# Attention with token and channel mixing on one core: third chunk's scores in plain float32, key and query splits and token-weight conversion moved

## The chip, the cores and the metric

The program runs on one core of one Trainium2 chip. A core has TensorE (PE, matrix products; its weight loads are listed as PEld), VectorE (DVE), ScalarE (ACT), GpSimd (POOL) and SyncE (SP, which here issues nearly all transfers). Each engine works through its own queue in the order in which the code issues to it, and waits at an instruction until what that instruction needs is there. The metric is the device time of one execution in microseconds (us).

## The reference

Three parts follow one another, for a batch of 2 and a sequence of 448. Attention with 12 heads of 64 mixes the heads before and after the softmax:

```
scores = scale * q @ k.T                      # per head
scores = einsum('bhij,hg->bgij', scores, w_pre)
attn   = exp(scores - max); attn = attn / (sum + 1e-9)
attn   = einsum('bhij,hg->bgij', attn, w_post)
x      = attn @ v                             # (2, 448, 768)
```

Then a mixer (`u = x + relu(x.T @ w_tok1) @ w_tok2` over the sequence, `x = u + relu(u @ w_ch1) @ w_ch2` over the channels), and a gated block with tanh gelu, a normalisation and a product over the sequence (`w_in`, `w_sg`, `w_out`). Inputs of attention are float32. The four mixer weights, `w_in` and `w_out` arrive as float64.

## The kernel before

**Numbers in two parts.** Most products are made of three: a float32 value is split into a high part in the type float32r (a cast) and a low part (the difference), and high*high, high*low, low*high are summed in PSUM (`mm3`, lines 626 to 631). The first scores of batch 0 are made otherwise, by one product of plain float32 operands.

**Attention in blocks.** Rows of the scores are taken in chunks of 120, 120, 120 and 88 for each batch, 8 chunks `(b, c)`. A chunk is worked in blocks of 10 rows by 12 heads (120 partitions), 90 blocks in all (12, 12, 12, 9 for each batch). For a block `i`: its scores come by DMA from the tile `S` into `P` (`b_dma`), ACT makes the high part `Ph` (`b_high`, line 391), POOL the low part `Pl` (`b_low`, line 397), PE multiplies by `w_pre` in three products (`b_pre`, 403 to 405), DVE takes the maximum `nm` (407), ACT the exponential `E` with its sum (411), DVE makes `rc` and its reciprocal `rr` (418, 421), POOL scales `w_post` by it into `wt` (424), PE multiplies `E` by `wt` in four products into `post` (436), and DVE copies that into `AT` (444).

**The order is written out by hand.** One loop runs over steps `i` from -8 to 89 (lines 555 to 612). Step `i` issues, for different blocks: `wt(i+1)`, the load of `P(i+8)`, `Ph(i+6)` and `Pl(i+6)`, `rc(i+2)`, the copy of `post(i-1)` to `AT`, `rr(i+2)`, then whatever the table `extra` holds for that step, then `pre(i+4)` and `post(i)`, and behind these the products `av` of a finished chunk with `v`, two heads' pairs at a time (lines 447 to 462, 588 to 592). So on POOL a step is `wt(i+1)`, `Pl(i+6)`, and the extras.

**The extras** are set by `add(step, ...)` (lines 509 to 548): the scores `qk` of the next chunk (345 to 365), the split of a pair of key heads into `KH` (DVE cast, 328) and `KL` (POOL, 329) by `kprep`, the split of three pairs of query heads into `QH` (DVE, 339) and `QL` (POOL, 340) by `qprep`, and loads. `load_const_late` issues a small DMA, builds the identity matrix `ident` on POOL (two instructions of masks.py) and a memset on DVE. A step with `qk` or `av` in it has more work for PE than one without.

**Weights.** `w_conv` (120 to 162) turns one piece of a float64 weight into two float32r parts. It is a generator: ACT takes `Abs` of the upper words into `cv` (117, issued one piece ahead by `w_abs`), DVE needs four instructions (135, 137, 139, 141), ACT casts to the high part (154 or 158) and DVE (156) or POOL (159) makes the low part; between them it yields. `pump(n)` advances it by `n` steps, as far as buffers allow. Pieces 0 and 1 are `w_tok1`, 2 and 3 `w_tok2`, from 4 on `w_ch1`. The load of piece `i+3` is issued when piece `i` is done, since there are three buffers `raw`. Pumping starts ten steps before the end of the loop, one step at a time, and goes on between the last six `av` of the tail loop (614 to 616).

**After the loop** `tok1(0)` and `tok1(1)` (660 to 678) multiply the transposed `x` by `w_tok1`; the transposes `xps` (PE, ACT cast 473 to `xh`, DVE 474 to `xl`) of batch 0 are made in the last four steps of the loop, those of batch 1 in `tok1(0)`. `rounds(n, w)` advances the waiting evacuations and pumps `w` each time. `tok2`, the channel mixing and the last block follow; `need(i)` pumps until a piece is ready.

Of the kernel before, what the change touches and what calls it, by code (L numbers as in the profile page):

```python
# [19 lines left out]
LD, LS, LP, LN = 8, 6, 4, 2  # L20
# [10 lines left out]
def tile_kernel(ctx, tc, q, k, v, w_pre, w_post, w_tok1, w_tok2, w_ch1, w_ch2,  # L31
# [88 lines left out]
    def w_conv(i):  # L120

        src, pr, a, n, scale, dst = pieces[i]
        r = wstate["raw"][i]
        if src.dtype == F32:
            f = r.bitcast(F32)
        else:

            r = r.rearrange("p a (n t) -> p a n t", t=2)
            lo, hi = r[:, :, :, 0], r[:, :, :, 1]
            if i not in wstate["abs"]:  # L130
                w_abs(i)
                yield
            f = wstate["abs"].pop(i)
            fi = f.bitcast(U32)
            nc.vector.tensor_scalar(f, f, MIN_HI, MAX_HI, op0=ALU.max, op1=ALU.min)
            yield
            nc.vector.tensor_scalar(fi, fi, 3, 0x3FFFFFFF, op0=ALU.logical_shift_left, op1=ALU.bitwise_and)
            yield
            nc.vector.scalar_tensor_tensor(fi, lo, 29, fi, op0=ALU.logical_shift_right, op1=ALU.bitwise_or)  # L139
            yield  # L140
            nc.vector.scalar_tensor_tensor(fi, hi, 0xC0000000, fi, op0=ALU.bitwise_and, op1=ALU.bitwise_or)  # L141

            w_abs(i + 1)
        yield
        if dst is None:
            h = wpool.tile([P, WC], F32R, tag="wth", name=f"wh{i}", bufs=WB)
            l = wpool.tile([P, WC], F32R, tag="wtl", name=f"wl{i}", bufs=WB)
            dst = pieces[i][5] = (h[:pr, :a * n].rearrange("p (a n) -> p a n", a=a),
                                  l[:pr, :a * n].rearrange("p (a n) -> p a n", a=a))
        elif callable(dst):  # L150
            dst = pieces[i][5] = dst()
        if i in p_t1:

            nc.scalar.copy(dst[0], f)
            yield
            nc.vector.tensor_tensor(dst[1], f, f32(dst[0]), op=ALU.subtract)
        elif scale is None:
            nc.scalar.copy(dst[0], f)  # L158
            nc.gpsimd.tensor_tensor(dst[1], f, f32(dst[0]), op=ALU.subtract)  # L159
        else:  # L160
            nc.scalar.activation(dst[0], f, AF.Copy, scale=scale)
            nc.vector.scalar_tensor_tensor(dst[1], f, scale, f32(dst[0]), op0=ALU.mult, op1=ALU.subtract)
# [134 lines left out]
    QG = 3  # L297
# [47 lines left out]
    def qk(b, c, i, pools=None, copies=(nc.scalar.copy, nc.scalar.copy)):  # L345

        s0, n = CH[c]
        if i == 0:
            SS[b, c] = big(f"S{b}_{c}", F32)[:120].rearrange("p (h s) -> p h s", h=H)
        ps = [pool.tile([P, 512], F32, tag=tag, name=f"qk{b}_{c}_{2 * i + j}")  # L350
              for j, (pool, tag) in enumerate(pools or [(psA, "A")] * 2)]
        cs = slice(i % QG * n, (i % QG + 1) * n)
        if b == 0 and (c < 2 or c == 2 and i < QG):

            terms = [(qn[b, c, i // QG], KX[b, i])]
        else:
            (qh, ql), (kh, kl) = QQ[b, c, i // QG], KK[b, i]
            terms = [(qh, kh), (qh, kl), (ql, kh)]
        for t, (x, y) in enumerate(terms):
            for j in range(2):  # L360
                rows = slice(64 * j, 64 * j + 64)
                nc.tensor.matmul(ps[j][:n, :S], lhsT=x[rows, cs], rhs=y[rows], start=(t == 0),  # L362
                                 stop=(t == len(terms) - 1))
        for j in range(2):
            copies[j](SS[b, c][:n, 2 * i + j, :], ps[j][:n, :S])
# [112 lines left out]
    def add(step, fn, *a):  # L478
        extra.setdefault(step, []).append((fn, a))
# [29 lines left out]
    for i in range(NP):  # L509
# [3 lines left out]
        else:  # L513
            add(2 * i - 9, qk, 0, 1, i)

        add(2 * i + 11 if i < QG else 3 * i - 5, kprep, 0, i, nc.vector.tensor_copy, nc.gpsimd)
    add(-LP, turn_over, 4)
    add(6, qprep, 0, 2, 1)
    for g in range(NQ):
        add(1 + 6 * g, load_q, 0, 3, g)  # L520
    for hp in range(NP):
        add(3 + hp, load_v, 0, hp)
    add(LD + 2, load_const_late)

    for x in range(2, NCH):
        b, c = chunks[x]
# [4 lines left out]
        for i in range(NP):  # L531
# [5 lines left out]
            else:  # L537
                add(s_, qk, b, c, i)
            if nxt and i % QG == QG - 1:
                add(s_ + 3, qprep, *nxt, i // QG)  # L540
                if nxt2:
                    add(s_ + 4, load_q, *nxt2, i // QG)
            if nxt and nxt[1] == 0:
# [4 lines left out]
                add(s_ + 1 + i % 2, kprep, nxt[0], i, nc.vector.tensor_copy, nc.gpsimd)  # L548

    todo = []  # L550
    NS = S // KP
    X, RX = {}, {}
    turns = [(0, s, ch) for ch in range(2) for s in range(NS)]

    for i in range(-LD, NB):
# [25 lines left out]
        if i >= 0:  # L581
# [3 lines left out]
                b_turn(i)  # L585

            nb = len(chunk_blocks(CH[c][1]))
            while todo and NP - len(todo) < 2 * ((j + nb // 6) * 3 // nb):
                av(*todo[0])
                if todo[0][1] == len(CH) - 1 and b:  # L590
                    add(i + 1, load_v, b, todo[0][2])
# [16 lines left out]
        if i + LP >= NB:  # L608
            for _ in range(2):
                turn(psB.tile([P, 512], F32, tag="B", name=f"xps0_{len(turns)}"), *turns.pop(0))  # L610
        if i + LS + 4 >= NB:

            pump(1)
    while todo:
        av(*todo.pop(0))
        pump(2)
    actx.close()


# [37 lines left out]
    with ExitStack() as mctx:  # L657
        mp = mctx.enter_context(tc.tile_pool(name="tok", bufs=1, reuse_waits="tile"))
        RR = {}
        def tok1(b, turns=()):  # L660
# [4 lines left out]
            for tt in range(TOK // P):  # L665
                ts = slice(tt * P, (tt + 1) * P)
                for ch in range(2):
# [5 lines left out]
                    for _ in range(2):  # L673
                        if turns:
                            s, tch = turns.pop(0)
                            turn(bank(f"xps1_{s}_{tch}"), 1, s, tch)
                    rounds(2, 2 - b)
            RR[b] = (rh, rl, got)

        def tok2(b):  # L680
# [305 lines left out]
```

## Time and profile before

| | |
|---|---|
| time, median of 3 runs | 553.54 us (553.32 to 556.22) |
| profiled execution, its own time | 552.82 us |
| its span | 550.9 us |
| PE busy | 537.3 us, 98% (3630 products) |
| PE weight loads busy | 477.5 us, 87% |
| DVE, ACT, POOL busy | 394.8 (72%), 274.0 (50%), 280.8 us (51%) |
| granted TensorE clock, mean | 0.999 of full speed |

The page counts an engine as busy while it executes. The share is an average over the whole program; the stretches by stage are read from the rows further down. A product in float32 stands in the profile as two records, so the four products of `post` are 8 records, and a pair of plain score products for one pair of heads is 4.

### The profile page before, as it was taken

To read this page: it belongs to the slowest core of one execution; us is meant where nothing else is said; L and a number is where in the kernel's file an instruction comes from. 1 tells how busy PE (TensorE), PEld (TensorE's weight loads), DVE (VectorE), ACT (ScalarE), POOL (GpSimd) and SP (SyncE) were. 2 spreads that over 40 slices of the span, in tenths; PEclk is the share of its full clock that TensorE was granted. 3 is DMA by queue.
4 is the path that set the end of the run, shared out by engine and by line. 5 is a ranking of instruction groups with operands and counts; after the bars stand their busy time and mean duration, and the time that the engine had idled before them with its cause. 6 is when DMAs were issued, how large, how long until landed. Compare 5 with 4: busy or idle time off the path is not lost.

```text
span 550.9 us, 10089 instructions
## 1 busy us (share of the span) xinstructions
PE 537.3 (98%) x3630; PEld 477.5 (87%) x3630; DVE 394.8 (72%) x789; ACT 274.0 (50%) x582; POOL 280.8 (51%) x295
## 2 busy tenths in 40 slices
PE   9999999999999999789999999999999999999997
PEld 5677888888888888789999999999999998888986
DVE  4787877667676677886356876778887974798972
ACT  4875757666676765454333443433233343455320
POOL 0699997767676763035522223244444545057600
PEclk9999999999999999999999999999999999999999
DMA  6564444424422541342032434334353323201322
GB/s 204 187 209 143 149 141 108 123 81 149 157 100 97 165 125 35 125 147 75 0 113 71 142 97 150 117 114 153 115 166 102 96 90 111 67 1 47 106 101 101
DMA packets 26340, 63.12 MB, mean 115 GB/s; under 512 B 2914, under 2 KB 18834, under 8 KB 26290
## 3 DMA queue, kind: packets, MB, share of 16 engines
q1 hardware_dynamic: 26002, 62.10, 34.5%
q8 instruction: 29, 0.48, 0.3%
q10 hardware_dynamic: 288, 0.37, 0.2%
q14 instruction: 21, 0.17, 0.1%
HBM read 40.36 MB, written 2.75 MB: 78 GB/s over the span
## 4 chain that ended last, share of the span: by engine, by line
PE 85%; DVE 6%; issue 2%; POOL 2%; ACT 2%; DMA 1%; SPq 0%; POOLq 0%; ACTq 0%
PE post L436 11%; PE av L454 7%; PE qk L362 5%; PE c1ps L630 5%; PE c2ps L630 5%; PE c2ps L629 5%; PE c1ps L629 5%; PE c2ps L631 5%; PE c1ps L631 5%; PE pre L403 4%; PE pre L405 3%; PE pre L404 3%; PE ups L629 2%; PE ups L631 2%; PE ups L630 2%
## 5 line engine op out<-in xcount | busy, mean ns | idle before, releaser
L397 POOL TENSOR_TENSOR Pl<-P,Ph 120x448 fp32r<-120x448 f32 x87 | 100.2, 1152 | 54.7 <-ACT Ph L391 51.7
L159 POOL TENSOR_TENSOR wl<-cv,wh 128x768 fp32r<-128x768 f32 x28 | 52.5, 1875 | 122.3 <-ACT wh L158 88.1
L436 PEld LDWEIGHTS post<-wt,E 120*112 120x112 f32 x720 | 86.2, 176 | 7.9 <-POOL wt L424 3.2
L436 PE MATMUL post<-wt,E 120*112 120x120 f32 x720 | 88.8, 266 | 2.2 <-POOL wt L424 1.5
L411 ACT ACTIVATE E<-pre,nm 120x448 f32<-120x448 f32 x90 | 57.5, 638 | 55.4 <-DVE rc L418 45.6
L444 DVE COPY AT<-post 112x480 f32<-112x480 f32 x90 | 58.6, 651 | 6.0 <-PE post L436 1.6
L407 DVE TENSOR_REDUCE nm<-pre 120x1 f32<-120x448 f32 x90 | 54.9, 610 | 4.1 <-PE pre L405 2.9
L139 DVE SCALAR_TENSOR_TENSOR cv<-raw,cv 128x768 uint32<-128x768 uint32 (+3 forms) x44 | 54.0, 1227 | 1.2
L630 PE MATMUL c1ps<-ul,wh 128*128 128x448 f32 x144 | 52.9, 367 | 0.0
L630 PE MATMUL c2ps<-r1l,wh 128*128 128x448 f32 x144 | 52.9, 367 | 0.0
L391 ACT CAST Ph<-P 120x448 fp32r<-120x448 f32 x90 | 52.2, 580 | 0.9 <-DMA P<-S 0.8
L629 PE MATMUL c1ps<-uh,wh 128*128 128x448 f32 x144 | 52.3, 363 | 0.0
L629 PE MATMUL c2ps<-r1h,wh 128*128 128x448 f32 x144 | 52.3, 363 | 0.0
L631 PE MATMUL c1ps<-uh,wl 128*128 128x448 f32 x144 | 52.0, 361 | 0.0
L631 PE MATMUL c2ps<-r1h,wl 128*128 128x448 f32 x144 | 52.0, 361 | 0.0
L117 ACT ACTIVATE cv<-raw 128x768 f32<-128x768 f32 (+3 forms) x44 | 36.2, 823 | 27.4 <-POOL wl L159 18.3
L454 PE MATMUL av<-AT,vn 112*64 112x120 f32 (+1 forms) x768 | 42.0, 263 | 0.3 <-DVE xT L462 0.3
L158 ACT CAST wh<-cv 128x768 fp32r<-128x768 f32 x28 | 23.4, 836 | 36.6 <-DVE cv L141 32.8
L403 PE MATMUL pre<-Ph,wpl 120*120 120x448 f32 x90 | 40.5, 450 | 0.6 <-DVE rc L418 0.4
L141 DVE SCALAR_TENSOR_TENSOR cv<-raw,cv 128x768 uint32<-128x768 uint32 (+3 forms) x44 | 40.2, 914 | 1.1
L454 PEld LDWEIGHTS av<-AT,vn 112*64 112x64 f32 x768 | 37.1, 137 | 3.1 <-PE av L454 0.5
L652 DVE SCALAR_TENSOR_TENSOR r1l<-c1ps,r1h 128x448 fp32r<-128x448 f32 x24 | 15.0, 624 | 31.2 <-ACT r1h L650 31.2
(202 smaller groups left out, 1220.3 us busy)
## 6 DMA issues: line engine op xcount, KB each, us to landing
P<-S SPq DMA_DIRECT2D x90, 210.0 KB
raw<-in_w_ch_dram SPq DMA_DIRECT2D x24, 768.0 KB
raw<-in_w_v_dram SPq DMA_DIRECT2D x6, 512.0 KB
raw<-in_w_u_dram SPq DMA_DIRECT2D x4, 768.0 KB
raw<-in_w_out_dram SPq DMA_DIRECT2D x6, 512.0 KB
vn<-in_v_dram SPq DMA_DIRECT2D x12, 224.0 KB
out_dram<-xT SPq DMA_DIRECT2D x12, 224.0 KB
qn<-in_q_dram SPq DMA_DIRECT2D x10, 180.0 KB
```

What stands on the lines that cost most here:

```text
L139: nc.vector.scalar_tensor_tensor(fi, lo, 29, fi, op0=ALU.logical_shift_right, op1=ALU.bitwise_or)
L159: nc.gpsimd.tensor_tensor(dst[1], f, f32(dst[0]), op=ALU.subtract)
L397: eng.tensor_tensor(lo, st[i]["P"], f32(st[i]["h"]), op=ALU.subtract)
L403: nc.tensor.matmul(ps[:BW, :S], lhsT=wpl, rhs=hi, start=True, stop=False)
L407: nc.vector.tensor_reduce(out=nm, in_=ps[:BW, :S], axis=AX.X, op=ALU.max, negate=True)
L411: nc.scalar.activation(e, ps[:BW, :S], AF.Exp, bias=nm, scale=1.0, accum_out=sm)
L436: nc.tensor.matmul(ps[:KP, r * BW:(r + 1) * BW], lhsT=e[:, r * KP:(r + 1) * KP], rhs=wt, start=True, stop=True)
L444: nc.vector.tensor_copy(AT[b, c][:, :, :, j * IB:(j + 1) * IB], src)
L454: nc.tensor.matmul(ps[64 * j:64 * j + 64, :cols], lhsT=vn[b, hp][:, j, r, :], rhs=AT[b, c][:, r, 2 * hp + j, :cols], start=(r == 0), stop= ...
L629: nc.tensor.matmul(ps, lhsT=lh, rhs=rh, start=(start and i == 0), stop=False)
L630: nc.tensor.matmul(ps, lhsT=lh, rhs=rl, start=False, stop=False)
L631: nc.tensor.matmul(ps, lhsT=ll, rhs=rh, start=False, stop=(stop and i == n - 1))
```

## The change

In the scores of chunk `(0, 2)`, the three pairs of heads 3 to 5 are now made by one product of plain float32 operands each, as those of 0 to 2 already were (`qk`: `c < 3`). The query split `qprep(0, 2, 1)` is gone. The key splits of batch 0 (`kprep`), which stood at steps 11, 13, 15, 4, 7, 10 for heads' pairs 0 to 5, stand at 5, 9, 15, 17, 21, 23. The query splits of chunk `(0, 3)` move from 12 and 16 to 13 and 19, `load_const_late` from 10 to 27.

The conversion of the token weights starts earlier: three pump steps ahead of the `av` of a step, from step 75 on (75, 79, 83, 86, 89), two in each of the last four steps, and none between the last six `av`. Pieces 2 to 5 have one more yield ahead of their ACT cast. In `tok1(0)` a round pumps once, not twice.

```
--- before.py
+++ after.py
@@ -142,6 +142,9 @@
 
             w_abs(i + 1)
         yield
+        if p_t2[0] <= i <= p_c1[1]:
+
+            yield
         if dst is None:
             h = wpool.tile([P, WC], F32R, tag="wth", name=f"wh{i}", bufs=WB)
             l = wpool.tile([P, WC], F32R, tag="wtl", name=f"wl{i}", bufs=WB)
@@ -350,7 +353,7 @@
         ps = [pool.tile([P, 512], F32, tag=tag, name=f"qk{b}_{c}_{2 * i + j}")
               for j, (pool, tag) in enumerate(pools or [(psA, "A")] * 2)]
         cs = slice(i % QG * n, (i % QG + 1) * n)
-        if b == 0 and (c < 2 or c == 2 and i < QG):
+        if b == 0 and c < 3:
 
             terms = [(qn[b, c, i // QG], KX[b, i])]
         else:
@@ -513,14 +516,15 @@
         else:
             add(2 * i - 9, qk, 0, 1, i)
 
-        add(2 * i + 11 if i < QG else 3 * i - 5, kprep, 0, i, nc.vector.tensor_copy, nc.gpsimd)
+    for s_, i in [(5, 0), (9, 1), (15, 2), (17, 3), (21, 4), (23, 5)]:
+        add(s_, kprep, 0, i, nc.vector.tensor_copy, nc.gpsimd)
     add(-LP, turn_over, 4)
-    add(6, qprep, 0, 2, 1)
     for g in range(NQ):
+        add(13 + 6 * g, qprep, 0, 3, g)
         add(1 + 6 * g, load_q, 0, 3, g)
     for hp in range(NP):
         add(3 + hp, load_v, 0, hp)
-    add(LD + 2, load_const_late)
+    add(27, load_const_late)
 
     for x in range(2, NCH):
         b, c = chunks[x]
@@ -537,7 +541,8 @@
             else:
                 add(s_, qk, b, c, i)
             if nxt and i % QG == QG - 1:
-                add(s_ + 3, qprep, *nxt, i // QG)
+                if x > 2:
+                    add(s_ + 3, qprep, *nxt, i // QG)
                 if nxt2:
                     add(s_ + 4, load_q, *nxt2, i // QG)
             if nxt and nxt[1] == 0:
@@ -548,6 +553,10 @@
                 add(s_ + 1 + i % 2, kprep, nxt[0], i, nc.vector.tensor_copy, nc.gpsimd)
 
     todo = []
+
+    def av_due():
+        return todo and NP - len(todo) < 2 * ((j + nb // 6) * 3 // nb)
+
     NS = S // KP
     X, RX = {}, {}
     turns = [(0, s, ch) for ch in range(2) for s in range(NS)]
@@ -585,7 +594,10 @@
                 b_turn(i)
 
             nb = len(chunk_blocks(CH[c][1]))
-            while todo and NP - len(todo) < 2 * ((j + nb // 6) * 3 // nb):
+            if i > LAST + 3 and av_due():
+
+                pump(3)
+            while av_due():
                 av(*todo[0])
                 if todo[0][1] == len(CH) - 1 and b:
                     add(i + 1, load_v, b, todo[0][2])
@@ -608,12 +620,9 @@
         if i + LP >= NB:
             for _ in range(2):
                 turn(psB.tile([P, 512], F32, tag="B", name=f"xps0_{len(turns)}"), *turns.pop(0))
-        if i + LS + 4 >= NB:
-
-            pump(1)
+            pump(2)
     while todo:
         av(*todo.pop(0))
-        pump(2)
     actx.close()
 
 
@@ -674,7 +683,7 @@
                         if turns:
                             s, tch = turns.pop(0)
                             turn(bank(f"xps1_{s}_{tch}"), 1, s, tch)
-                    rounds(2, 2 - b)
+                    rounds(2)
             RR[b] = (rh, rl, got)
 
         def tok2(b):
```

On POOL, about steps 10 to 12 (`wt12` is for block 12, `Pl17` for block 17, `KL0_5` is the low part of batch 0's last pair of key heads), the program before has

```order
L424 TENSOR_SCALAR wt11_606<-wd_post_68,rr11_575 120x120
L397 TENSOR_TENSOR Pl16_612<-P16_538,Ph16_610 120x448
L329 TENSOR_TENSOR KL0_5_620<-kn0_3_105,KH0_5_619 128x448
masks.py:197 MEMSET ident_72 128x128
masks.py:199 AFFINE_SELECT ident_72<-ident_72 128x128
L424 TENSOR_SCALAR wt12_642<-wd_post_68,rr12_617 120x120
L397 TENSOR_TENSOR Pl17_648<-P17_566,Ph17_646 120x448
```

and the changed one

```order
L427 TENSOR_SCALAR wt11_598<-wd_post_68,rr11_567 120x120
L400 TENSOR_TENSOR Pl16_604<-P16_530,Ph16_602 120x448
L427 TENSOR_SCALAR wt12_624<-wd_post_68,rr12_609 120x120
L400 TENSOR_TENSOR Pl17_630<-P17_558,Ph17_628 120x448
L427 TENSOR_SCALAR wt13_650<-wd_post_68,rr13_635 120x120
L400 TENSOR_TENSOR Pl18_656<-P18_600,Ph18_654 120x448
```

The key split and the identity matrix that stood ahead of `wt12` are gone from there.

On POOL, about steps 23 to 25, the program before has

```order
L424 TENSOR_SCALAR wt24_1116<-wd_post_68,rr24_1077 120x120
L397 TENSOR_TENSOR Pl29_1122<-P29_1022,Ph29_1120 120x448
L329 TENSOR_TENSOR KL1_3_1130<-kn1_1_979,KH1_3_1129 128x448
L424 TENSOR_SCALAR wt25_1150<-wd_post_68,rr25_1127 120x120
L397 TENSOR_TENSOR Pl30_1156<-P30_1068,Ph30_1154 120x448
L340 TENSOR_TENSOR QL1_0_0_1164<-qn1_0_0_720,QH1_0_0_1163 128x360
L424 TENSOR_SCALAR wt26_1181<-wd_post_68,rr26_1161 120x120
```

and the changed one

```order
L427 TENSOR_SCALAR wt24_1090<-wd_post_68,rr24_1051 120x120
L400 TENSOR_TENSOR Pl29_1096<-P29_992,Ph29_1094 120x448
L332 TENSOR_TENSOR KL0_5_1104<-kn0_3_105,KH0_5_1103 128x448
L332 TENSOR_TENSOR KL1_3_1108<-kn1_1_949,KH1_3_1107 128x448
L427 TENSOR_SCALAR wt25_1128<-wd_post_68,rr25_1101 120x120
L400 TENSOR_TENSOR Pl30_1134<-P30_1042,Ph30_1132 120x448
L343 TENSOR_TENSOR QL1_0_0_1142<-qn1_0_0_694,QH1_0_0_1141 128x360
L427 TENSOR_SCALAR wt26_1159<-wd_post_68,rr26_1139 120x120
```

A split of batch 0's keys (`KL0_5`) now stands ahead of one of batch 1's (`KL1_3`); `KL0_3`, `QL0_3_1` and `KL0_4` have come in ahead of these rows, at steps 17, 19 and 21.

On ACT, behind the loop's last transposes (`xh0` of `xps0_1`), the copies of the last `av` results to `xT` stood in the program before as

```order
L473 CAST xh0_3467<-xps0_1_3558 112x384
L459 COPY xT_66<-av1_3_0_3565 128x8x10
L462 COPY xT_66<-av1_3_0_3565 128x8
L117 ACTIVATE cv2_3577<-raw2_3132 128x448
L154 CAST t1_2h_3579<-cv1_3405 112x512
L459 COPY xT_66<-av1_3_2_3597 128x8x10
L462 COPY xT_66<-av1_3_2_3597 128x8
L117 ACTIVATE cv3_3622<-raw3_3482 128x448
L158 CAST t2_0h_3624<-cv2_3577 128x448
L459 COPY xT_66<-av1_3_4_3630 128x8x10
L462 COPY xT_66<-av1_3_4_3630 128x8
L117 ACTIVATE cv4_3656<-raw4_3594 128x768
```

and stand in the changed one as

```order
L476 CAST xh0_3463<-xps0_1_3566 112x384
L117 ACTIVATE cv4_3574<-raw4_3478 128x768
L462 COPY xT_66<-av1_3_0_3576 128x8x10
L465 COPY xT_66<-av1_3_0_3576 128x8
L462 COPY xT_66<-av1_3_2_3598 128x8x10
L465 COPY xT_66<-av1_3_2_3598 128x8
L462 COPY xT_66<-av1_3_4_3620 128x8x10
L465 COPY xT_66<-av1_3_4_3620 128x8
L659 ACTIVATE xh0_3463<-t1ps0_0_0_3662 128x384
```

The `Abs` and casts of the token weights no longer stand between the copies; the `Abs` of piece 4, the first of `w_ch1`, now stands ahead of the first of them.

## Rows read from the trace of the kernel before

**Rows 1.** Waits of PE: waiting line, releaser; us in total, times, longest.
```profile
PE t1ps L629 <- ACT xT L462: 2.5, 1, 2.5
PE t1ps L629 <- ACT xh L473: 1.8, 1, 1.8
```
**Rows 2.** Busy time by stretch: PE, PEld, DVE, ACT, POOL, clock, DMA share, GB/s.
```profile
212.90:227.90 15.00, 14.30 (x216) 13.04 (x216) 12.35 (x31) 7.64 (x21) 1.10 (x3) 1.00 0.16 46
227.90:230.40 2.50, 0.00 (x0) 0.00 (x0) 2.43 (x9) 0.97 (x4) 0.14 (x1) 1.00 0.63 240
```
**Rows 3.** PE in time order, steps 3 to 14: start, us, instruction, [idle before].
```profile
26.28 0.98 PE L436 MATMUL post<-wt,E 120*112 120x120 f32 x8
...
27.71 0.98 PE L436 MATMUL post<-wt,E 120*112 120x120 f32 x8
28.62 1.77 PE L362 MATMUL qk<-kn,qn 64*120 64x448 f32 x8
30.32 0.46 PE L403 MATMUL pre<-Ph,wpl 120*120 120x448 f32 x1
...
33.89 0.98 PE L436 MATMUL post<-wt,E 120*112 120x120 f32 x8
...
35.81 1.07 PE L436 MATMUL post<-wt,E 120*112 120x120 f32 x8 [0.34 <-POOL wt L424]
...
41.94 0.98 PE L436 MATMUL post<-wt,E 120*112 120x120 f32 x8
...
44.72 1.07 PE L436 MATMUL post<-wt,E 120*112 120x120 f32 x8 [1.19 <-POOL wt L424]
45.72 0.47 PE L362 MATMUL qk<-KH,QH 64*120 64x448 f32 x2
...
47.13 0.47 PE L403 MATMUL pre<-Ph,wpl 120*120 120x448 f32 x1
...
47.85 0.98 PE L436 MATMUL post<-wt,E 120*112 120x120 f32 x8
...
49.56 1.07 PE L436 MATMUL post<-wt,E 120*112 120x120 f32 x8
```
**Rows 4.** POOL in time order, steps 18 to 20 and 25.
```profile
59.50 0.50 POOL L424 TENSOR_SCALAR wt<-wd_post,rr 120x120 f32<-120x120 f32 x1
60.21 1.14 POOL L397 TENSOR_TENSOR Pl<-P,Ph 120x448 fp32r<-120x448 f32 x1 [0.21 <-ACT Ph L391]
61.31 1.16 POOL L329 TENSOR_TENSOR KL<-kn,KH 128x448 fp32r<-128x448 f32 x1
62.44 0.38 POOL L424 TENSOR_SCALAR wt<-wd_post,rr 120x120 f32<-120x120 f32 x1
...
75.80 0.96 POOL L340 TENSOR_TENSOR QL<-qn,QH 128x360 fp32r<-128x360 f32 x1
76.73 0.38 POOL L424 TENSOR_SCALAR wt<-wd_post,rr 120x120 f32<-120x120 f32 x1
```
**Rows 5.** PE in time order, `post` of blocks 19 and 26.
```profile
62.32 0.98 PE L436 MATMUL post<-wt,E 120*112 120x120 f32 x8
...
77.47 0.98 PE L436 MATMUL post<-wt,E 120*112 120x120 f32 x8
```
**Rows 6.** DVE in time order, steps 83 to 85, and in the tail.
```profile
209.50 0.38 DVE L459 COPY xT<-av 128x120 f32<-128x120 f32 x1 [1.98 <-PE av L454]
209.72 0.68 DVE L139 SCALAR_TENSOR_TENSOR cv<-raw,cv 112x512 uint32<-112x512 uint32 x1
...
230.45 1.44 DVE L139 SCALAR_TENSOR_TENSOR cv<-raw,cv 128x448 uint32<-128x448 uint32 x1
```
**Rows 7.** PE in time order, `post` of block 86.
```profile
212.99 1.05 PE L436 MATMUL post<-wt,E 120*112 120x120 f32 x8 [0.50 <-DVE rr L421]
```
**Rows 8.** ACT in time order, from the tail to `tok1(0)`.
```profile
229.62 0.56 ACT L158 CAST t_0h<-cv 128x448 fp32r<-128x448 f32 x1 [1.52 <-DVE cv L141]
...
245.06 0.83 ACT L158 CAST wh<-cv 128x768 fp32r<-128x768 f32 x1 [1.29 <-DVE cv L141]
```

More of the change, by code (lines that the diff above doesn't have):

```diff
@@ L144, in w_conv @@
         yield
+        if p_t2[0] <= i <= p_c1[1]:
+            yield
         if dst is None:
@@ L352, in qk @@
         cs = slice(i % QG * n, (i % QG + 1) * n)
-        if b == 0 and (c < 2 or c == 2 and i < QG):
+        if b == 0 and c < 3:
             terms = [(qn[b, c, i // QG], KX[b, i])]
@@ L514, in tile_kernel @@
             add(2 * i - 9, qk, 0, 1, i)
-        add(2 * i + 11 if i < QG else 3 * i - 5, kprep, 0, i, nc.vector.tensor_copy, nc.gpsimd)
+    for s_, i in [(5, 0), (9, 1), (15, 2), (17, 3), (21, 4), (23, 5)]:
+        add(s_, kprep, 0, i, nc.vector.tensor_copy, nc.gpsimd)
     add(-LP, turn_over, 4)
-    add(6, qprep, 0, 2, 1)
     for g in range(NQ):
+        add(13 + 6 * g, qprep, 0, 3, g)
         add(1 + 6 * g, load_q, 0, 3, g)
@@ L522, in tile_kernel @@
         add(3 + hp, load_v, 0, hp)
-    add(LD + 2, load_const_late)
+    add(27, load_const_late)
     for x in range(2, NCH):
@@ L539, in tile_kernel @@
             if nxt and i % QG == QG - 1:
-                add(s_ + 3, qprep, *nxt, i // QG)
+                if x > 2:
+                    add(s_ + 3, qprep, *nxt, i // QG)
                 if nxt2:
@@ L550, in tile_kernel, with av_due @@
     todo = []
+    def av_due():
+        return todo and NP - len(todo) < 2 * ((j + nb // 6) * 3 // nb)
     NS = S // KP
@@ L587, in tile_kernel @@
             nb = len(chunk_blocks(CH[c][1]))
-            while todo and NP - len(todo) < 2 * ((j + nb // 6) * 3 // nb):
+            if i > LAST + 3 and av_due():
+                pump(3)
+            while av_due():
                 av(*todo[0])
@@ L610, in tile_kernel @@
                 turn(psB.tile([P, 512], F32, tag="B", name=f"xps0_{len(turns)}"), *turns.pop(0))
-        if i + LS + 4 >= NB:
-            pump(1)
+            pump(2)
     while todo:
         av(*todo.pop(0))
-        pump(2)
     actx.close()
@@ L676, in tok1 @@
                             turn(bank(f"xps1_{s}_{tch}"), 1, s, tch)
-                    rounds(2, 2 - b)
+                    rounds(2)
             RR[b] = (rh, rl, got)
```

## Prediction

> **What bounds the kernel.** I read the granted clock first (full speed nearly throughout, so no term here is about the clock), then the page's busy shares, then the waits of PE, then busy time by stretch, and last the queues in time order where PE stops. PE is busy 98% of the span; the reader is to see there that time can only come from PE's own work or from the few places where it stands still. The waits name two large ones, 2.5 and 1.8 us, both at the first products of the token mixing [rows 1]. In the stretch ahead of them PE works 14.30 of 15.0 us and then not at all for 2.5, while DVE is busy 12.35 of 15.0 and 2.43 of 2.5 [rows 2]. So DVE is the engine waited for around the end of attention. The rest of attention is set by PE, except where POOL's `wt` is late early on: in time order `post` waits for it three times in steps 8 to 14 [rows 3].
>
> **Third chunk's scores (PE).** Two pairs of heads in plain float32 take from 28.62 to the next product at 30.32, 1.70 us or 0.85 for a pair; two in three split products from 45.72 to 47.13, 1.41 or 0.705 [rows 3]. Three pairs change, so PE gets 3 x 0.145 = 0.44 us more. The plain form was measured in this place on the same shapes; I take it as it is. Term: +0.44.
>
> **Three waits that go.** A step without scores or `av` is 27.71 - 26.28 = 1.43 us from `post` to `post`. Blocks 8, 12 and 14 come 1.92, 2.78 and 1.71 us after the one before, 0.49 + 1.35 + 0.28 = 2.12 too late, and after each PE takes some 0.09 longer to start again (44.72 to 45.72 against 27.71 to 28.62) [rows 3]. Sum 2.39. Ahead of `wt8` POOL had a query split, ahead of `wt12` a key split and the identity matrix, ahead of `wt14` a query split; all of these leave those places. What comes late next there is nothing that I can find: a POOL step is `Pl` 1.10 (60.21 to 61.31) and `wt` about 0.35, together 1.45 [rows 4], as long as PE's 1.43, and the splits that remain stand in steps that scores make 1.7 us longer. The cost left is 0 to 2.39; I take it all as gone. Term: -2.39.
>
> **New waits later.** The moved splits are not gone but come in steps 15 to 23, where those of batch 1 stand already. A key split holds POOL 1.13 (61.31 to 62.44), a query split 0.93 (75.80 to 76.73), the smaller one of chunk (0, 3) about 0.7 by its columns [rows 4]. From the end of `wt19` to that of `wt26` POOL now has 7 steps, 10.15, 6 key splits, 6.78, and 0.7 + 0.93: 18.6 us. Before it had two key splits and the small one less, 15.6, and needed 17.1, from 59.50 + 0.50 to 76.73 + 0.38 [rows 4], so 1.5 went on waits for ACT and DVE and on longer instructions. PE needs 77.47 - 62.32 = 15.15 from `post` of block 19 to that of 26 [rows 5]. POOL's lead at block 19 was 62.32 - 60.00 = 2.32 [rows 4, 5]. It will be larger, since POOL has 4.0 us less to do up to there and PE is only 2 earlier, but `wt` can't run ahead of `rr`, which DVE makes behind an older `post`. With a lead of 2.9 and 0.5 of the 1.5, block 26 waits 18.6 + 0.5 - 15.15 - 2.9 = 1.0 us. About 0.3 more falls at block 30, since key splits 4 and 5 of batch 1 and now the identity matrix follow, and 0.1 on starting again. Bounds: a lead of 4 (a guess at where `rr` stops it) and nothing lost, no wait; a lead of 2.32 and all 1.5 lost, 2.8, with block 30 some 3.2. I take the middle. Term: +1.4.
>
> Behind `KL0_5` on SP stands the load of batch 1's keys into the buffer that it reads, and behind that the load of `P` of block 32. It is some 3 us late at most, and its block is nine steps ahead of its `post`. No cost; without that cover a late `P` would hold ACT, and with it `E`.
>
> **End of attention.** From 212.9 to 230.4 PE has 14.3 us of work and stands still for 3.2 [rows 2]. The last `av` results are copied by ACT and DVE, and both queues hold conversions ahead of these copies: ACT stood 1.52 us at a cast that waits for DVE's conversion, and the copy behind it is what the first token product waited for [rows 8, 1]. In the change DVE has three conversion instructions less in this stretch and none between the last copies: of its 14.8 us about 13.3 remain. That is still close to PE's 14.3, and it comes in bursts: each of the last steps has two `xl`, an `AT` copy and one to four conversions, and a transpose can't start until the `xl` three transposes back is done. So I let PE wait 1.6 in the transposes and ahead of the last `av`, half of the 3.2 (bounds 0 and 3.2), and 0.2 at the first token product: 16.1 in place of 17.5, -1.4. The 0.50 at block 86, which waits for DVE [rows 7], also goes, with 0.1 of starting again, since the two long conversions of steps 84 and 85 are no longer there. The conversions moved to steps 75, 79 and 83 are two or three DVE instructions each, the longer kind 0.68 us, so at most some 1.4; they stand where DVE is idle until `av` is done, 1.98 us [rows 6]. If that cover were gone, the next maximum and exponential would be late by as much. Term: -2.0 (0 to -3.8).
>
> **Token mixing.** The 1.8 us goes back to ACT, which stands at the cast of a channel weight (1.29 us idle until DVE's conversion is done [rows 8]) with the transposes' casts behind it. With one pump in place of two DVE has two conversions at most in a pass of PE. The casts that need them stand in a later pass, since the extra yield puts a cast one pump later. The slower pace leaves piece 6 unfinished when the channel mixing starts, which needs it only at its third group. I take 1.8 and 0.2 for the second wait behind it (bounds -1.0 and -2.4). Term: -2.0.
>
> **Sum.** 0.44 - 2.39 + 1.4 - 2.0 - 2.0 = -4.55 us. Made against the profiled execution's own 552.82 us this is 548.3. That execution is 0.7 below the median of 553.54, and the time to foretell is a median: 549.0.
>
> **Rivals.** POOL's debt is the full one: lead 2.32, all 1.5 lost, +3.2 in place of +1.4, 550.8. For it: POOL has more work than PE has time from block 19 to 26 whatever its lead. Against: its total up to block 26 is smaller than before. Chance 0.14.
>
> No new wait at all, because of just that: -5.95, 547.6. For it speaks also that before no `post` waited behind block 14 in this part. Chance 0.19.
>
> DVE's conversions and POOL hold each other up. One conversion instruction with two inputs in SBUF took 1.44 us, where that line on a longer tile took 0.68 [rows 6]; POOL was making a token weight's low part meanwhile. At step 79 two such stand beside POOL's `Pl`; if each waits for one (1.10 [rows 4]), ACT's cast, its `av` copy and the next `Ph` are 2.2 late, and if POOL's lead takes up 0.6 of it, 1.6 comes to PE: 550.6. Chance 0.14. The Trainium skill has this as a rule, in SBUF — State Buffer, "Who interferes with whom": a VectorE instruction with both inputs in SBUF and a GpSimd one that reads SBUF exclude each other for their whole length, and the first to issue wins. By that rule, with which the 1.44 agrees, this rival would be the forecast; I hold it lower because DVE would have to come second each time, and no row tells which of the two is first there.
>
> Slower: ACT's `Abs` of piece 4 now stands ahead of the last three `av` copies on ACT, and its load can only start when DVE has read piece 1 for the last time, in step 86. That is some 9 us earlier: PE's 14.3 us of work there [rows 2] less about 4 for the last `av` and 1 for what precedes DVE's read. A load that takes longer than this delays the copies, the last `av` and the token mixing one for one; it would have to take some 14 us to eat the gain and 16 to be slower by 0.5%. For it: ACT can't pass it. Against: DMA has little to do there, with a share of 0.16 [rows 2]. 556.3, chance 0.03.
>
> **How the numbers follow.** Forecast 549.0 with 0.50, its own range 547.3 to 550.6. 0.5% of the time, about what can be told from no change, is 2.77 us, so faster means under 550.8. It holds nearly all of the forecast, the second rival, and half of the first and third: 0.49 + 0.19 + 0.07 + 0.07, taken as 0.80; slower 0.03; same 0.17. With every term at its good end (-7.6) it is 545.9; two bad ends together give 552.6. I take 546.0 to 551.8.
>
> **What would show it.** Plain scores: 1.70 us for steps 9 and 13 each. Waits gone: `post` of 8, 12 and 14 at 1.43 us, or what scores leave. New waits: `post` of 26 and 30 waiting for `wt`. End: the wait of the first token product under 0.5 us, single waits of transposes on DVE's `xl` instead. Token mixing: no wait of PE on ACT's `xh` over 0.3 us. I am wrong if the 2.5 us wait only moves into the transposes, or if `post` waits over 2 us in steps 20 to 31.

## The result and the profile after

The changed kernel takes 548.90 us (median of 5 executions, 548.57 to 549.15), the kernel before 553.54 beside it (553.29 to 556.22): ratio 0.9896, 95% interval 0.9872 to 0.9920. The forecast was 549.0. The profiled execution took 548.57 with a span of 546.5, 4.4 less than before.

The table gives PE's time, read from the order of its instructions, for the four stretches that the change touches: from the first `post` to that of block 17, on to block 31, from block 82 to the first token product (`t1ps`), and on to the second token product (`t2ps`). The rows below the second are the experiments.

| kernel | 0 to 17 | 17 to 31 | 82 to t1ps | t1ps to t2ps | median us |
|---|---|---|---|---|---|
| before | 36.64 | 32.69 | 25.56 | 22.08 | 553.54 |
| changed | 34.65 | 35.60 | 23.98 | 19.45 | 548.90 |
| e1b: front alone | 34.65 | 35.58 | 25.57 | 25.93 | 555.93 |
| e2: tail alone | 36.62 | 32.70 | 24.07 | 19.58 | 548.37 |
| e8: extra yield alone | 36.64 | 32.70 | 23.47 | 21.36 | 549.51 |
| e9: changed, no extra yield | 34.65 | 35.56 | 24.86 | 19.60 | 550.20 |
| e7: changed, old places of conversions | 34.65 | 35.58 | 23.47 | 19.61 | 548.72 |
| e4: changed, old pace | 34.65 | 35.55 | 24.00 | 21.42 | 551.33 |
| e3: changed, 3 key splits early | 34.65 | 33.35 | 24.13 | 19.58 | 547.06 |
| e5: changed, 5 key splits early | 34.65 | 32.89 | 24.06 | 19.58 | 545.92 |
| e6: e5, split products | 34.68 | 32.89 | 24.07 | 19.58 | 546.76 |
| e10: e5, old places of conversions | 34.65 | 32.85 | 23.47 | 19.60 | 545.57 |
| e11: e10, split products | 34.25 | 32.86 | 23.47 | 19.60 | 545.97 |

The stretches in between agree within 0.05 us in all of them. Two do not belong to any edit and differ from execution to execution: the start up to the first `post` (19.98 to 21.04) and the last part from the channel mixing's second product on (192.4 to 193.0). So a stretch of one profiled execution at the full clock settles a tenth of a microsecond, where the medians of 4 to 10 executions settle about half of one. The experiments ran on three chips (e1 to e4; e5 to e7 and e1b; e8 to e11), with the kernel before beside them on each: its medians there are 555.18, 555.32 and 555.43. One execution of e1 (887.43 us, the profiled one, so that e1 has no row) and one of e4 (1075.25 us) lie far from all others and are left out of the medians and ratios.

First, the waits of PE after (waiting line, releaser; us in total, times, longest):

```profile
PE post L439 <- POOL wt L427: 1.1, 3, 0.8
PE idle L506 <- DVE ident L501: 1.0, 1, 1.0
PE xps L473 <- DVE xl L477: 1.0, 2, 0.7
PE pre L408 <- POOL Pl L400: 0.6, 1, 0.6
PE t1ps L638 <- DVE xT L465: 0.5, 1, 0.5
```

The 2.5 and the 1.8 us of [rows 1] are gone. In their place are single waits of the transposes and 0.5 us at the first token product, and `post` waits for POOL again.

PE in time order in steps 7 to 14 (start, us, instruction, [idle before]), which answers to [rows 3]:

```profile
33.39 0.98 PE L439 MATMUL post<-wt,E 120*112 120x120 f32 x8
...
34.82 0.98 PE L439 MATMUL post<-wt,E 120*112 120x120 f32 x8
35.73 1.77 PE L365 MATMUL qk<-kn,qn 64*120 64x448 f32 x8
37.42 0.46 PE L406 MATMUL pre<-Ph,wpl 120*120 120x448 f32 x1
...
41.00 0.98 PE L439 MATMUL post<-wt,E 120*112 120x120 f32 x8
...
42.42 0.98 PE L439 MATMUL post<-wt,E 120*112 120x120 f32 x8
...
45.74 0.98 PE L439 MATMUL post<-wt,E 120*112 120x120 f32 x8
...
47.17 0.98 PE L439 MATMUL post<-wt,E 120*112 120x120 f32 x8
```

Blocks 8, 12 and 14 follow the one before at 1.43, 1.42 and 1.43 us: the three waits are gone. Then PE at blocks 19 to 30, which answers to [rows 5]:

```profile
59.84 0.98 PE L439 MATMUL post<-wt,E 120*112 120x120 f32 x8
...
73.39 0.44 PE L365 MATMUL qk<-KL,QH 64*88 64x448 f32 x2 [0.28 <-POOL KL L332]
...
77.35 1.07 PE L439 MATMUL post<-wt,E 120*112 120x120 f32 x8 [0.81 <-POOL wt L427]
...
87.09 1.07 PE L439 MATMUL post<-wt,E 120*112 120x120 f32 x8 [0.18 <-POOL wt L427]
```

Rows 59.84 and 77.35 are blocks 19 and 26: 17.51 us, where before took 15.15 [rows 5]. At 73.39 PE waits for a key split itself. POOL over the same blocks, `wt19` and `wt26` first and last, as in [rows 4]:

```profile
57.10 0.50 POOL L427 TENSOR_SCALAR wt<-wd_post,rr 120x120 f32<-120x120 f32 x1
...
72.07 2.38 POOL L332 TENSOR_TENSOR KL<-kn,KH 128x448 fp32r<-128x448 f32 x2
...
76.79 0.50 POOL L427 TENSOR_SCALAR wt<-wd_post,rr 120x120 f32<-120x120 f32 x1
```

From the end of one to that of the other POOL takes 77.29 - 57.60 = 19.69 us, of which it stands idle for 0.2, with two key splits back to back ahead of the scores of step 25. Last, PE at the end of attention, which answers to [rows 7] and the waits of [rows 2]:

```profile
211.59 1.80 PE L439 MATMUL post<-wt,E 120*112 120x120 f32 x16
...
219.84 0.54 PE L473 MATMUL xps<-ident,xT 128*112 128x128 f32 x3 [0.71 <-DVE xl L477]
...
225.69 2.10 PE L457 MATMUL av<-AT,vn 112*64 112x90 f32 x48 [0.28 <-DVE xT L462]
227.96 0.84 PE L457 MATMUL av<-AT,vn 112*64 112x90 f32 x16 [0.17 <-DVE xT L465]
229.30 0.41 PE L638 MATMUL t1ps<-xh,t_0h 112*128 112x384 f32 x1 [0.51 <-DVE xT L465]
```

Blocks 85 and 86 run as one piece, without the 0.50 us of [rows 7], and no wait in this part is above 0.71.

### The profile page after: what moved, and what is told of

The parts are those of the page before. It is cut to its first block, busy times and chain, and to the rows that moved or that the text cites. A ratio compares the mean times of both kernels' runs of the same rounds, so it can differ in the third digit from the quotient of the medians.

```text
span 546.5 us, 10076 instructions
## 1 busy us (share of the span) xinstructions
PE 537.0 (98%) x3624; PEld 476.4 (87%) x3624; DVE 397.3 (73%) x788; ACT 274.1 (50%) x582; POOL 282.1 (52%) x294
## 4 chain that ended last, share of the span: by engine, by line
PE 92%; DVE 3%; DMA 2%; POOL 1%; issue 1%; ACT 0%; SPq 0%; POOLq 0%; DVEq 0%
PE post L439 12%; PE av L457 6%; PE qk L365 6%; PE c2ps L638 5%; PE c1ps L638 5%; PE c1ps L640 5%; PE c2ps L640 5%; PE c2ps L639 5%; PE c1ps L639 5%; PE pre L406 4%; PE pre L408 3%; PE pre L407 3%; PE ops L640 2%; PE ops L639 2%; PE ups L640 2%; PE ups L639 2%
## 5 line engine op out<-in xcount | busy, mean ns | idle before, releaser
L117 ACT ACTIVATE cv<-raw 128x768 f32<-128x768 f32 (+3 forms) x44 | 36.2, 822 | 26.6 <-POOL wl L162 19.1
L427 POOL TENSOR_SCALAR wt<-wd_post,rr 120x120 f32<-120x120 f32 x90 | 35.6, 396 | 2.6 <-DVE rr L424 1.4
```

## The experiments

**Front and tail apart.** e1 and e1b are the kernel before with the front of the change only, e2 the same with the tail only.

```diff
 e1, e1b: the edits of the scores, kprep, qprep and load_const_late
 e2:      the edits of w_conv, av_due, pump(3), pump(2) and rounds(2)
```

> The kernel before with only the first half of the change: plain scores, moved key and query splits, later identity; the conversions are as before. Theory: the two traces put the front of attention (score term, three waits gone, new waits in steps 21 to 30) at +0.9 us from the first post to that of block 31, so this kernel is slower than before: 554.4 us (553.9 to 555.0), with PE waiting for wt and KL in steps 21 to 30 as in the changed kernel. Rival 1, the terms as forecast (+0.44, -2.39, +1.4): 553.0. Rival 2, the front is where the gain comes from: 550 to 551.5.

> The kernel before with only the second half of the change: conversions moved, the extra yield, the slower pace in the token mixing; the front is as before, with its three waits for wt at blocks 8, 12 and 14. Theory: the end of attention (-1.6) and the token mixing (-2.6) are the whole gain: 549.3 by these two, 548.0 if the front costs what the traces say (+0.9) and the changed kernel is 548.9. Rival 1, the front as forecast: 549.5 or more. Rival 2, the front is where the gain comes from: 551 to 552.

> Again the kernel before with only the first half of the change, for a profile that can be read: its first one was of a disturbed execution. From the first post to that of block 31 its PE should take 70.2 us as in the changed kernel (before: 69.3), with waits for wt and KL in steps 21 to 30. What is open: executions of this kernel and of the kernel before show mean clocks of 0.990 to 0.996 where kernels with the new end of attention show 0.999 to 1.000. Theory: the clock falls behind PE's stop of 2.5 us at the first token product. Rival: it falls elsewhere, at the start or the end of the program, and has nothing to do with the change.

The front alone is slower: 556.61 and 555.93 us against 555.18 and 555.32 of the kernel before beside them, ratios 1.0023 (1.0005 to 1.0041) and 1.0019 (1.0000 to 1.0039). These intervals hardly leave 1; executions with the same mean clock are further apart (at 0.996, e1 took 554.45 to 554.78 us and before beside it 553.22 to 553.51). In the profiles the first two stretches take 70.23 us where before takes 69.33: the plain scores and the new waits cost 0.9 more than the three waits gave. The tail alone is 548.37, ratio 0.9883 (0.9861 to 0.9905), so it carries the whole gain. Its stretches are 4.0 us shorter than those of before; that the medians are 6.8 apart has to do with the clock of the kernel before, whose executions at 0.999 took only 552.7 to 553.2. The absolute numbers forecast for e1 were missed, since on these chips most executions of the kernel before took longer; e1b's profile shows how that can come about. Busy time by stretch of e1b (PE, PEld, DVE, ACT, POOL, clock, DMA share, GB/s):

```profile
213.00:228.00 15.00, 14.31 (x216) 13.04 (x216) 12.34 (x30) 7.63 (x20) 1.10 (x3) 1.00 0.16 45
228.00:231.00 3.00, 0.50 (x2) 0.50 (x3) 2.93 (x10) 0.93 (x4) 0.68 (x1) 0.74 0.67 229
231.00:234.00 3.00, 3.00 (x11) 3.00 (x11) 1.57 (x2) 0.94 (x1) 0.47 (x1) 0.50 0.81 264
234.00:237.00 3.00, 3.00 (x15) 2.89 (x14) 1.02 (x2) 1.92 (x4) 0.00 (x0) 0.62 0.64 233
237.00:249.00 12.00, 10.68 (x68) 10.23 (x66) 10.21 (x17) 6.47 (x13) 3.58 (x3) 1.00 0.25 76
249.00:252.00 3.00, 2.70 (x9) 2.45 (x10) 2.84 (x5) 1.42 (x3) 1.23 (x1) 0.66 0.57 221
252.00:255.00 3.00, 3.00 (x15) 3.00 (x15) 1.68 (x4) 1.90 (x4) 0.99 (x1) 0.77 0.31 76
```

The clock is the third number from the right. PE stands for 2.5 us ahead of 230.5, the granted clock falls to 0.50 (the lower level, 1.2 GHz) and is back at 1.00 from 237 on. The mean of 0.74 over 228 to 231 puts the fall at about 229.4 (an estimate, for a single fall), so it came while PE still stood. The clock falls again within 249 to 255, behind the second stop (1.5 us, for `xh`). The profiled execution of before had stops at the same two places (2.5 and 1.8 us, [rows 1]) and stayed at 1.00. So the way from `t1ps` to `t2ps` is 25.93 us here and 22.08 there, 3.85 apart, with the same instructions in the same order. In this execution the theory holds, and the rival (a fall elsewhere) doesn't. Of the other executions only the mean clock is known, not where it fell.

**The pace of the token mixing.**

```diff
-                    rounds(2)
+                    rounds(2, 2 - b)
```

> The changed kernel with the old pace of conversions in the first token product (two pumps in a round in place of one); all else as changed. Theory: the slower pace is what removed PE's wait for xh; that wait comes back with 1.8 to 2.6 us: 550.7 to 551.5. Rival, the extra yield of the conversion or the earlier conversions at the end of attention removed it: 548.6 to 549.4, with no wait of PE on xh.

551.33 us, ratio to before 0.9935 (0.9911 to 0.9959): the time is what the theory said, and it is the pace that matters. The way from `t1ps` to `t2ps` is 21.42, 1.97 more than in the changed kernel, nearly all of it one wait in time order of PE:

```profile
245.45 0.44 PE L639 MATMUL t1ps<-xl,t_2h 112*128 112x384 f32 x1 [1.66 <-DVE xl L477]
```

That is not the wait that the theory named: PE stands for `xl` of DVE, while ACT had cast the `xh` by 243.60. DVE in time order has that `xl` behind a conversion:

```profile
243.97 0.96 DVE L141 SCALAR_TENSOR_TENSOR cv<-raw,cv 128x768 uint32<-128x768 uint32 x1
244.84 1.02 DVE L477 TENSOR_TENSOR xl<-xps,xh 112x384 fp32r<-112x384 f32 x2
```

**The end of attention.** e7 puts the conversions back to their old places and keeps the extra yield and the pace.

```diff
-            if i > LAST + 3 and av_due():
-                pump(3)
...
-            pump(2)
+        if i + LS + 4 >= NB:
+            pump(1)
     while todo:
         av(*todo.pop(0))
+        pump(2)
```

> The changed kernel with the conversions of the last steps of attention where they were before (one pump in each of the last steps, two behind each last product with v, none ahead of av); the extra yield and the slower pace in the token mixing stay. Theory: the end of attention alone is worth 1.6 us from the post of block 82 to the first token product: 550.5 to 551.1 us, with the wait of the first token product for ACT's xT back at some 2.3 us. Rival 1, the pace of the token mixing carries most of it: 549.0 to 549.7. Rival 2, PE's long stop there also lowers the granted clock behind it: 551.2 to 553, with a mean clock under 0.998.

My theory fell: 548.72 us, ratio to before 0.9880 (0.9861 to 0.9898), as fast as with the moved conversions, and from block 82 to `t1ps` PE takes 23.47 us, 0.5 less than in the changed kernel. The 2.5 us stop went without any conversion being moved. What was left was the extra yield; e8 is that alone, in the kernel before, and e9 the changed kernel without it.

```diff
 e8: +        if p_t2[0] <= i <= p_c1[1]:
     +            yield
 e9: -        if p_t2[0] <= i <= p_c1[1]:
     -            yield
```

> The kernel before with one part of the change alone: the extra yield, which puts ACT's cast of a converted piece one pump later. On ACT the first 128x448 cast then stands behind the last copy of the products with v and no longer ahead of it. Theory, formed from the run with the old conversions at the end of attention: this one cast, waiting for DVE with the last copy behind it, was the 2.5 us wait of the first token product; post of block 82 to that product falls from 25.6 to 23.5 us, and time to 550.4 to 551.2 us, with the mean clock at 0.998 or more. Rival, DVE's amount of conversions in the last steps (the reason as forecast): no gain at the end of attention, 553 to 555.5.

> The changed kernel without the extra yield: the 128x448 casts stand on ACT ahead of the last three copies of the products with v again, while DVE's conversions stay early and at the slower pace. Theory (the place of the cast on ACT decides): a wait of the first token product for ACT's xT comes back in part, 549.5 to 551 us. Rival (the earlier conversions are enough without it): 548.5 to 549.2.

One `yield` takes the kernel before to 549.51 us, ratio 0.9906 (0.9885 to 0.9926), and the rival is out. That is 0.9 below the forecast range, which had nothing for the 0.72 us that the yield gives in the token mixing. ACT in time order shows how the end of attention gains. In before the first of the last two copies stood behind the cast of 229.62 [rows 8]:

```profile
230.09 0.29 ACT L459 COPY xT<-av 128x80 f32<-128x80 f32 x1
```

In e8 the same copies stand ahead of that cast:

```profile
227.22 0.29 ACT L462 COPY xT<-av 128x80 f32<-128x80 f32 x1
227.33 0.20 ACT L465 COPY xT<-av 128x8 f32<-128x8 f32 x1
228.85 0.57 ACT L161 CAST t_0h<-cv 128x448 fp32r<-128x448 f32 x1 [1.33 <-DVE cv L141]
```

ACT still stands 1.33 us at the cast, but the copies are done by then. In the token mixing PE now waits for `xl`, as in e4, and no longer 1.8 us for `xh`:

```profile
243.71 0.45 PE L633 MATMUL t1ps<-xl,t_2h 112*128 112x384 f32 x1 [1.48 <-DVE xl L477]
```

In e9 the time came as the theory had it, 550.20 us, ratio 0.9922 (0.9897 to 0.9946), though with two executions of six at a mean clock of 0.996 and 0.997 (551.59 and 552.11 us). The wait that the theory named did not come: the first token product waits for nothing. PE in e9 stands ahead of it, at the last products with v:

```profile
226.67 0.84 PE L454 MATMUL av<-AT,vn 112*64 112x90 f32 x16 [0.93 <-DVE xT L459]
228.36 2.08 PE L454 MATMUL av<-AT,vn 112*64 112x90 f32 x48 [0.85 <-DVE xT L462]
```

DVE in e9 in time order has a conversion right ahead of each of the copies that PE waits for:

```profile
225.71 0.63 DVE L139 SCALAR_TENSOR_TENSOR cv<-raw,cv 128x448 uint32<-128x448 uint32 x1
226.25 0.36 DVE L459 COPY xT<-av 128x120 f32<-128x120 f32 x1
...
227.38 0.61 DVE L141 SCALAR_TENSOR_TENSOR cv<-raw,cv 128x448 uint32<-128x448 uint32 x1
227.91 0.29 DVE L459 COPY xT<-av 128x80 f32<-128x80 f32 x1
```

By these rows it is DVE's queue that decides once the conversions are moved. The yield helps there too (24.86 to 23.98); that it does so by putting the conversions of the piece behind it one pump later is likely, but no run shows it apart. Without the yield the moved conversions are worth 25.56 - 24.86 = 0.7 us; with it they cost 0.5.

**POOL's work in the front.** e3 makes three key splits on POOL while it is idle ahead of block 0, e5 five, and e5 makes the identity matrix in step 45.

```diff
+    for i in range(3):                      # e5: range(5)
+        kprep(0, i, nc.gpsimd.tensor_copy, nc.gpsimd)
-    for s_, i in [(5, 0), (9, 1), (15, 2), (17, 3), (21, 4), (23, 5)]:
+    for s_, i in [(5, 3), (9, 4), (15, 5)]: # e5: [(5, 5)]
```

> The changed kernel with key splits 0 to 2 of batch 0 made wholly by POOL (copy and subtraction) while it stands idle ahead of block 0, and splits 3, 4 and 5 in steps 5, 9 and 15. Theory: the waits of steps 21 to 30 come from POOL's amount of work in steps 15 to 23, three splits (3.4 us) of which are now gone from there: the 2.9 us of new waits go but for some 0.3, and time is 546.3 us (545.8 to 546.9). Rival 1, these waits come from DVE and POOL holding each other up or from longer POOL instructions and not from the amount: 548.4 to 549.2. Rival 2, POOL's early work delays DVE's score copies at the start (both read SBUF or write it at once) by 1 us or more: 547.3 to 549.

> The kernel with three early key splits, now with splits 0 to 4 made by POOL ahead of block 0, split 5 in step 5, and the identity matrix made in step 45 in place of 27. Theory (what is late in steps 20 to 31 is POOL's amount of work): the last wait there, 0.5 us at block 30, goes, and time is 546.5 us (546.1 to 546.9) where three early splits gave 547.06. Rival 1, that wait belongs to batch 1's key splits 4 and 5 alone: 546.9 to 547.2. Rival 2, five early splits (1.7 us each, from 4.95 us on) run to 13.6 us and into the first Pl at 15.3 or DVE's work there: 547.5 or more.

e3 takes 547.06 us, 0.2 above its range, ratio to before 0.9857 (0.9833 to 0.9881): blocks 17 to 31 take 33.35, 2.25 less than in the changed kernel. One wait is left, at block 30:

```profile
84.90 1.07 PE L439 MATMUL post<-wt,E 120*112 120x120 f32 x8 [0.32 <-POOL wt L427]
```

In e5 it is gone: 32.89, and 545.92 us, 0.2 below its range, ratio 0.9830 (0.9812 to 0.9848). So the waits were POOL's amount of work in steps 15 to 27. POOL in e3 shows what an early split costs:

```profile
4.95 0.56 POOL L331 CAST KH<-kn 128x448 fp32r<-128x448 f32 x1 [4.53 <-DMA kn<-in_k_dram]
5.59 1.13 POOL L332 TENSOR_TENSOR KL<-kn,KH 128x448 fp32r<-128x448 f32 x1
6.67 0.56 POOL L331 CAST KH<-kn 128x448 fp32r<-128x448 f32 x1
7.30 1.13 POOL L332 TENSOR_TENSOR KL<-kn,KH 128x448 fp32r<-128x448 f32 x1
```

1.72 us for a split in time that nobody wanted; the second rivals of both runs (a later start) are not seen, with the first `post` at 20.41 and 20.02.

**Split products for the third chunk, and the old places.** e6 is e5 with the last three pairs in split products and their query split in step 6; e10 is e5 with the old places of the conversions; e11 is e10 with split products, with four early key splits (the other two in steps 5 and 9) and the query split made early on POOL too.

```diff
 e6, e11: -        if b == 0 and c < 3:
          +        if b == 0 and (c < 2 or c == 2 and i < QG):
 e6:      +    add(6, qprep, 0, 2, 1)
 e11:     +    qprep(0, 2, 1, nc.gpsimd.tensor_copy)
```

> The same kernel with five early splits, but with the last three pairs of heads of the third chunk in split products again, as before the change, and its query split in step 6. Theory: the plain scores cost 0.145 us a pair, and POOL has room for the query split now: 0.4 us less than with plain scores, 546.1 us (545.8 to 546.5). Rival, the query split makes block 8 wait for wt again (0.49 + 0.09 us before): no gain, 546.5 to 546.9.

> Five key splits made early by POOL, the identity matrix in step 45, the extra yield and the slower pace, but the conversions at the end of attention at their old places. Theory: moving the conversions cost 0.5 to 0.6 us between the post of block 82 and the first token product (23.98 in the changed kernel, 23.47 with the old places), so this is below 545.92: 545.3 us (545.0 to 545.6). Rival, the difference was one of single executions: 545.8 to 546.1.

> As the kernel with five early key splits and the old places at the end of attention, but POOL makes four key splits and the query split of the third chunk ahead of block 0, key splits 4 and 5 come in steps 5 and 9, and the third chunk's last three pairs are in split products. Theory: split products save 0.145 us a pair, and with the query split out of POOL's steps nothing waits for it: 0.4 us less than with plain scores, 544.9 us (544.5 to 545.2). Rival, the query split ends behind 15.3 us and holds the first Pl, or steps 5 to 12 wait for wt: 545.3 or more.

e6: 546.76 us (545.60 to 547.06), ratio 0.9837 (0.9817 to 0.9856): no gain, as its rival said; the first stretch is 34.68, so the three pairs gave 0.4 and a wait of block 8 for `wt` took it (1.78 us behind block 7 in place of 1.43). e11 has the query split out of the way, and that stretch is 34.25, 0.40 less: plain scores cost what the forecast said. Its median, 545.97 (545.18 to 546.25), ratio 0.9839 (0.9815 to 0.9864), does not show it and lies with its rival; its profiled start was 20.80 where e10's was 20.02, as much as starts differ elsewhere. By the time the two are not told apart. e10, 545.57 us (544.96 to 546.05), ratio 0.9836 (0.9811 to 0.9860), is the fastest by median, 3.3 below the changed kernel's 548.90; against e5, which ran on another chip, the difference is no more than the spread, and the 0.6 rests on the stretch (24.06 to 23.47).

## Why the prediction came out

The total was right, to 0.1 us, and that closeness is luck. Of its five terms the first two held, and the last nearly; the new waits were twice the forecast, the end of attention had nearly its size but another cause, and the step from the profile to the median failed. These errors offset one another, with a part that was no work of the change.

**Plain scores, +0.44: right.** The first two pairs of scores with a changed one among them start at 35.73, and the next `pre` comes 1.69 us later, where I had read 1.70 for two plain pairs; e11 takes 0.40 back.

**Three waits gone, -2.39: right.** With the scores, -1.95 up to block 17; measured 34.65 - 36.64 = -1.99.

**New waits later, +1.4: mis-sized, it is +2.9** (35.60 - 32.69). The way of working it out holds with the measured numbers: POOL needed 19.69 us where I had 19.1, and its lead at block 19 was 59.84 - 57.60 = 2.24 where I had let it grow to 2.9; 19.69 - 15.15 - 2.24 = 2.3, against the 2.36 that blocks 19 to 26 took more. The rest falls up to block 31. So the lead was the first rival's, and of its 1.5 us of loss 1.1 came (19.69 - 18.6). That rival's sum, done again, is 18.6 + 1.5 - 15.15 - 2.32 = 2.6, or 3.0 with block 30 and starting again, where I wrote 2.8 and 3.2; so the 2.9 is nearly all of it. That POOL had less to do in total, which I held against it, did not matter: in the steps ahead POOL could not use the time to work ahead, but stood 0.52, 0.51, 1.00 and 0.61 us for `Ph` (ahead of its rows at 32.69, 40.29, 47.90 and 50.00). What I did not name is that the scores themselves can wait for a key split, the 0.28 at 73.39.

**End of attention, -2.0: size nearly right (23.98 - 25.56 = -1.6), cause wrong.** I took the wait for a matter of how much DVE has to convert, and credited the moved conversions. But DVE's work there did not fall from 14.8 to 13.3 us: from block 86 to the first token product it was busy for 14.82 us before and for 14.76 in the changed kernel. The runs show the place of one cast on ACT: the yield alone gives 23.47 - 25.56 = -2.1, the move on top of it +0.5. The row was there, the cast at 229.62 with the copy behind it [rows 8], and I had noted in the token mixing that the yield puts a cast one pump later; I did not ask where that puts this cast. The 0.50 at block 86 did go, as said, with the conversions of steps 84 and 85, and waits of 0.31 and 0.71 us came in the transposes, where before had one of 0.29. The first token product waits 0.51, about the limit that I had named.

**Token mixing, -2.0: right in the main, and -2.6 (19.45 - 22.08).** The pace gives 1.97 (e4), the yield 0.72 more (e8: 21.36 - 22.08), which I had not counted on top. That `xh` waits behind ACT's cast was only the last link: with the yield alone the wait moves to `xl`, behind a conversion on DVE (1.48 us in e8, 1.66 in e4). What had to be spread was DVE's conversions, and the slower pace does that, as I had it.

**DVE and POOL excluding each other at step 79** did happen and cost nothing. DVE after, in time order:

```profile
199.80 0.90 DVE L139 SCALAR_TENSOR_TENSOR cv<-raw,cv 112x512 uint32<-112x512 uint32 x1
200.74 1.52 DVE L141 SCALAR_TENSOR_TENSOR cv<-raw,cv 112x512 uint32<-112x512 uint32 x1
```

Against 0.68 each alone [rows 6]. The Trainium skill (SBUF — State Buffer, "Who interferes with whom") has the rule, and the trace agrees with it. In e3 the same two took 0.71 and 0.69 and the stretch from block 71 to 82 was the same 21.67 us, so it did not reach PE. There only POOL was held up: its `wt` and `Pl` beside them took 0.87 and 1.61 us, where others of its rows take 0.37 and 1.14; in the changed kernel both engines were (POOL's took 0.81 and 1.59).

**The slower rival**, a late load of piece 4: no wait of the last copies on ACT for it appears.

**From the profile to the median, +0.7: wrong.** I carried it over to the changed kernel; there it is 0.33. The clock is the likely reason: of 43 executions of before beside the experiments, 4 had a mean of 0.999 and took 552.7 to 553.2 us, 9 had 0.996 or 0.997 (553.2 to 553.8) and 30 had 0.990 to 0.994 (554.6 to 557.1). For the five of before beside the changed kernel no clock is on record, but three took 553.3 to 553.5 and two 555.9 and 556.2, as the last two groups do. All executions of the changed kernel are at 0.999 or above. The profile that I forecast from was one of the few that didn't fall, and I took "full speed" for a trait of the kernel.

In profiled time the four stretches sum to -1.99 + 2.91 - 1.58 - 2.63 = -3.3. The start was 0.5 earlier and the last part and what follows it 0.6 shorter, which makes 4.4; no edit touches them, and they differ as much among the other runs, so I count them as chance. Against the stretches alone the forecast of -4.55 was 1.2 too optimistic. The medians are 4.64 apart even so, and part of that had no term in my sum: the lower clock of the kernel before. How much it is in this comparison no run shows. One more slip: the good ends of the five terms as I bounded them add up to -8.2 and not to -7.6.

## What to carry to other kernels

Where an engine waits for another at the end of a stage, read which single instruction stands ahead of the awaited one in its queue before counting work: one cast moved behind one copy gave 2.1 us, where moving the conversions gave 0.7 without that and cost 0.5 with it. Work that is moved off a busy place should go to time that is idle whatever happens (POOL ahead of the first block), since an engine whose inputs come step by step, as POOL's did here, could not bank what it saved early. Add to a stop of PE what the clock may charge for it afterwards, and look at the clock of several executions, not of the profiled one alone.

## What was not expected of the hardware

With a stop of 2.5 us behind 15 us in which PE was busy for 14.31, the clock fell to the lower level in e1b's profiled execution. With the same stop it stayed at 1.00 in that of before (14.30 of 15 us). The same kernel on the same chip took 552.9 to 556.8 us: on two of the three chips two executions of before each had a mean clock of 0.999 and the others 0.990 to 0.997, on the third all 17 had 0.991 to 0.996. Stops of 1.48 and 1.66 us in kernels without the longer one (e8, e4) left the mean clock at 0.998 to 1.000; e1b's second fall came behind a 1.5 us stop some 12 us after the first fall had ended. A long stop is not the whole account: two of e9's executions had 0.996 and 0.997, and its profiled one (1.000) shows no stop above 0.93 us at the end of attention or behind it. What decides between the executions stays open.

POOL's cast from float32 to float32r of 128x448 took 0.56 us, half of its subtraction of the same tile (1.13). Its work ahead of block 0 did not lengthen DVE's copies from PSUM beside it: six of them took 4.39 us with it (e3) and 4.38 without (the changed kernel).
